# A delta-rule scan and a Fourier mixing block on one core: the first batch put in program order, the weights' conversion rewritten and moved behind it

## The chip, the cores and the metric

The kernel runs on one core of a Trainium2 chip, with one launch. A core has five engines that this text names by the letters of the profile: PE (matrix multiply), PEld (its weight loads, which overlap the multiplies), DVE (vector), ACT (scalar and activation), POOL (GpSimd) and SP (the queue that starts most transfers). The metric is the device time of one execution in microseconds; the kernel before took 895.09 us, the median of three runs (893.43 to 897.38).

## The reference: what is computed

Two blocks, one after the other, all in float32 (the two weight matrices come in as float64).

```python
# block 1, for each of 4 batches and 8 heads, 768 tokens, 48 channels
k_n = k / (norm(k) + 1e-6)
for t in range(768):
    y[t]  = q[t] @ state                       # read before the update
    v_old = state^T k_n[t]
    state = state + beta[t] * outer(k_n[t], v[t] - v_old)
# bridge: heads side by side, x is (4, 768, 384)
# block 2
mixed = real(fft(fft(x, axis=1), axis=2))
u  = x + mixed
un = (u - mean(u)) / sqrt(var(u) + 1e-6)
out = u + relu(un @ w_ch1) @ w_ch2             # w_ch1 384x1536, w_ch2 1536x384
```

## The kernel before

The scan is done in chunks of 64 tokens. Two chunks make a tile g of 128 tokens; a batch has 6 tiles, so there are 24 tiles and 48 steps n of one chunk each. Four tiles make a round; inside a chunk the token-by-token recurrence is replaced by the inverse of a triangular matrix, and a round's 32x32 triangles (32 on each of 128 partitions) are inverted together on DVE. The parts are generators that hand over at each `yield`, so that the main loop can interleave them.

`pre_a(g)` transposes K and forms the products of keys; `invert(r)` inverts a round; `pre_b(g)` prepares the tile's operands; `step(g, c)` carries the state S through one chunk and at a tile's end writes x:

```python
def pre_a(g):
    # four transposes of K on PE, copied to KT by ACT
    # 32 products KT x KT into a PSUM pair, copied by ACT to G and GX
def invert(r):
    nc.gpsimd.memset(M, 0.0)
    nc.vector.transpose(A, G)                            # L286
    nc.scalar.activation(nrm, diag, ACT.Sqrt)            # L292
    for _ in range(2):                                   # two Newton steps of 5 operations
        max, reciprocal, mult, add, times 0.5            # L295 to L299
    ...                                                  # nT, bn with beta, A scaled, L300 to L308
    for j in range(W - 1):                               # W is 32
        nc.vector.tensor_tensor(t, A[...], M[...], op=mult)        # L314
        nc.vector.tensor_tensor(M[...], M[...], t, op=add)         # L317
        yield
    nc.vector.transpose(A, M); nc.vector.transpose(G, M)           # L320, L321
def pre_b(g):
    # Q transposed, copied to QT by ACT; POOL: V times nT, and MT from A        L337 to L343
    # one<-G,GX on PE, XM by ACT; pair<-QT,KT on PE, LQ by DVE                  L356, L368
    # one<-A,XM on PE, into MT by ACT; then WT and U0 from MT, K, V on PE, ACT  L380 to L398
def step(g, c):
    # PE: WT x S;  DVE: U = U0 - that             L416
    # PE: K x U;   DVE: S = S + that (or a copy)  L433, L435
    # at c == 1: x = Q S (ACT, L456) + LQ U (DVE, L465)
```

The weights are turned from float64 into float32 in six pieces of 128x1536 (three of `w1`, three of `w2`), by integer operations on the two words of each number. The buffers carry tags, and a tag's buffers are shared with other parts: `big` (2 buffers) with E and hT, `F` and `O` (1 each) with the Fourier part's F and O3:

```python
def weights():
    nxt = staged(0)                     # a 1.5 MB load into a "big" buffer
    for i, (_, dst) in enumerate(pieces):
        w64 = nxt
        if i + 1 < len(pieces): nxt = staged(i + 1)
        lo, hi = w64[:, :, 0], w64[:, :, 1]
        tmp = wk.tile([128, 2, DFF], I32, tag="F")       # man, exp
        low = wk.tile([128, DFF], I32, tag="O")
        # DVE: man = (hi << 3 & mask) | one               L213, L215
        # DVE: low = lo >> 8; man += low * 2**-44         L217, L218 (two inputs)
        # DVE: exp: shift and mask, subtract and max, min, shift   L222, L224, L226, L227
        # DVE: sign; exp |= sign                          L229, L231 (two inputs)
        nc.gpsimd.tensor_tensor(dst, man, exp, op=mult)  # L232
```

`fourier(b)` and `mlp(b)`:

```python
def fourier(b):
    E = wk.tile([128, 2, TH, DM], F32, tag="big", bufs=2)
    O3 = wk.tile([128, 2, TH, DM], F32, tag="O")
    # for t in 0..2: POOL: E from x tiles t and t+3 (L482, L483); DVE: six folds (L486 to L493)
    F = wk.tile([ND + 1, 4, SEQ], F32, tag="F")
    # pf: 48 products of E and O3 with the tables, copied to F by ACT
    # pb: 24 products of F with dtab, added to x by DVE, mean and variance per tile
def mlp(b):
    for g in range(3):                                   # two tiles of 128 tokens each
        # un = normalised x; transposed by PE (ptr) to unT
        hT = wk.tile([128, KF, GT * 128], F32, tag="big", bufs=2)
        # ph: 36 products with w1, relu by DVE or ACT into hT
        # po: 24 products with w2, added to x by DVE, stored
```

Transfers: K, Q and V come in four transfers a tile and tensor (64 tokens of 4 heads each); K has a ring of 7 tiles; beta comes in 32 transfers a round, started by POOL; the Fourier tables are started by ACT at the very beginning.

The main loop runs before the first step `pre_a` of four tiles, `invert(0)`, `pre_b(0)`, and then 48 steps with the other parts beside them, the weights in the first batch:

```python
for g in range(RL): drain(pre_a(g))
...
drain(invert(0)); load_qv(1); drain(pre_b(0))
side = weights()
for n in range(2 * NLT):
    live = [(step(g, c), 1)]
    # pre_a of the next round in its steps 0 to 3, invert of it in 4 to 6, pre_b(g + 1)
    if b == 0: live.append((part(side, 3), 1))
    ...
    run(live)
    if i == 2 * NL - 1:                 # a batch's last step
        if b == 0: drain(side)
        run([(fourier(b), 1)] + ([(side, 1)] if b > 0 else []))
        side, done = mlp(b), 0
drain(side)
```

The program is not run in the order in which it is written: a scheduler at build time, with times of its own, orders each engine's instructions and gives out the buffers.

Of the kernel before, what the change touches and what calls it, by code (L numbers as in the profile page):

```python
# [11 lines left out]
BF16 = mybir.dt.bfloat16  # L12
# [4 lines left out]
C = 64  # L17
L = 128
# [40 lines left out]
def kernel(  # L59
# [52 lines left out]
    Ks, Qs = [], []  # L112
    for i in range(RING):
        t = const.tile([128, 2, 4, 64], F32, name=f"K{i}")
        nc.gpsimd.memset(t[:, :, :, D:64], 0.0)
        Ks.append(t)
    for i in range(2):
        t = const.tile([128, 2, 4, 64], F32, name=f"Q{i}")
        nc.gpsimd.memset(t[:, :, :, D:64], 0.0)
        Qs.append(t)  # L120
# [3 lines left out]
    def fetch(dst, src, g):  # L124
        b, n = divmod(g, NL)
        for hh in range(2):
            for c in range(2):
                t0 = n * L + c * C
                nc.sync.dma_start(out=dst[hh * C:hh * C + C, c],
                                  in_=src[b, 4 * hh:4 * hh + 4, t0:t0 + C, :].rearrange(  # L130
                                      "j t d -> t j d"))

    def load_k(g):
        if g < NLT:
            fetch(Ks[g % RING][:, :, :, 0:D], k, g)

    def load_qv(g):
        if g < NLT:
            fetch(Qs[g % 2][:, :, :, 0:D], q, g)
            Vs[g] = wk.tile([128, 2, 4, D], F32, tag="V", bufs=2, name="V")  # L140
            fetch(Vs[g], v, g)
# [3 lines left out]
    def load_beta(r):  # L145

        if r * RL >= NLT:
            return
        t = wk.tile([128, W], F32, tag="beta", bufs=2, name="beta")
        for i in range(RL):  # L150
            b, n = divmod(RL * r + i, NL)
            for q4 in range(4):
                hh, blk = divmod(q4, 2)
                p0 = q4 * W + i * 8
                for c in range(2):
                    t0 = n * L + c * C + blk * W
                    nc.gpsimd.dma_start(out=t[p0 + 4 * c:p0 + 4 * c + 4],  # L157
                                        in_=beta[b, 4 * hh:4 * hh + 4, t0:t0 + W])
        betas[r] = t
# [3 lines left out]
    for g in range(RL):  # L163
        load_k(g)
    load_beta(0)
    load_qv(0)
# [9 lines left out]
    nc.scalar.dma_start(out=evt, in_=cn["even"].ap())  # L176
    nc.scalar.dma_start(out=odt, in_=cn["odd"].ap())
    nc.scalar.dma_start(out=dtab, in_=cn["dtab"].ap())

    half_n = const.tile([128, GT], F32, name="half_n")  # L180
    nc.gpsimd.memset(half_n, -0.5)

    def weights():
# [19 lines left out]
        nxt = staged(0)  # L203
        for i, (_, dst) in enumerate(pieces):
            w64 = nxt
            if i + 1 < len(pieces):
                nxt = staged(i + 1)
            lo, hi = w64[:, :, 0], w64[:, :, 1]
            tmp = wk.tile([128, 2, DFF], I32, tag="F", name="wtmp")
            man, exp = tmp[:, 0], tmp[:, 1]  # L210
            low = wk.tile([128, DFF], I32, tag="O", name="wlow")

            nc.vector.tensor_scalar(man, hi, 3, 0x007FFFF8, op0=ALU.logical_shift_left,  # L213
                                    op1=ALU.bitwise_and)
            nc.vector.tensor_scalar(man, man, 0x3F800000, None, op0=ALU.bitwise_or)  # L215
            yield
            nc.vector.tensor_scalar(low, lo, 8, None, op0=ALU.logical_shift_right)  # L217
            nc.vector.scalar_tensor_tensor(man.bitcast(F32), low, 2.0 ** -44, man.bitcast(F32),  # L218
                                           op0=ALU.mult, op1=ALU.add)
            yield  # L220

            nc.vector.tensor_scalar(exp, hi, 20, 0x7FF, op0=ALU.logical_shift_right,  # L222
                                    op1=ALU.bitwise_and)
            nc.vector.tensor_scalar(exp, exp, 896, 0, op0=ALU.subtract, op1=ALU.max)  # L224
            yield
            nc.vector.tensor_scalar(exp, exp, 255, None, op0=ALU.min)  # L226
            nc.vector.tensor_scalar(exp, exp, 23, None, op0=ALU.logical_shift_left)  # L227
            yield
            nc.vector.tensor_scalar(low, hi, 31, 31, op0=ALU.logical_shift_right,  # L229
                                    op1=ALU.logical_shift_left)  # L230
            nc.vector.tensor_tensor(exp, exp, low, op=ALU.bitwise_or)  # L231
            nc.gpsimd.tensor_tensor(dst.rearrange("p c f -> p (c f)"), man.bitcast(F32),  # L232
                                    exp.bitcast(F32), op=ALU.mult)
            yield
# [11 lines left out]
    def pre_a(g):  # L246

        K = Ks[g % RING]
# [3 lines left out]
        for i in range(4):  # L252
            c, jj = divmod(i, 2)
            tr(pt[:, 128 * i:128 * i + 128],
               K[:, c, 2 * jj:2 * jj + 2, :].rearrange("p j d -> p (j d)"), i == 0)
        nc.scalar.activation(KT.rearrange("p c j t -> p (c j t)"), pt, ACT.Copy)
# [5 lines left out]
        for i in range(4):  # L262
            c, jj = divmod(i, 2)
            for q4 in range(4):
                for jp in range(2):
                    hh, blk = divmod(q4, 2)
                    t0 = hh * C
                    rhs = KT[lo[jp], c, jj, t0:t0 + C]
                    if blk:
                        rhs = rhs.rearrange("p (b t) -> p b t", b=2)[:, ::-1, :]  # L270
                    mm(pg[q4 * W:q4 * W + W, jp, C * i:C * i + C],
                       KT[lo[jp], c, jj, t0 + blk * W:t0 + blk * W + W], rhs, i == 0)
# [7 lines left out]
    def invert(r):  # L280
# [10 lines left out]
        diag = A.rearrange(flat)[:, 0:W * W:W + 1]  # L291
        nc.scalar.activation(nrm, diag, ACT.Sqrt)  # L292
        for _ in range(2):

            nc.vector.tensor_scalar(nrm, nrm, 1e-19, None, op0=ALU.max)  # L295
            nc.vector.reciprocal(bn, nrm)
            nc.vector.tensor_tensor(bn, bn, diag, op=ALU.mult)
            nc.vector.tensor_tensor(nrm, nrm, bn, op=ALU.add)
            nc.vector.tensor_scalar(nrm, nrm, 0.5, None, op0=ALU.mult)  # L299
# [25 lines left out]
    def pre_b(g):  # L325

        r, li = divmod(g, RL)
        K, Q, KT, V = Ks[g % RING], Qs[g % 2], KTs.pop(g), Vs.pop(g)
        MTd, Md, nT = rounds[r]
# [3 lines left out]
        for i in range(4):  # L333
            c, jj = divmod(i, 2)
            tr(pt[:, 128 * i:128 * i + 128],
               Q[:, c, 2 * jj:2 * jj + 2, :].rearrange("p j d -> p (j d)"), i == 0)
        nc.scalar.activation(QT.rearrange("p c j t -> p (c j t)"), pt, ACT.Copy)  # L337
# [21 lines left out]
        LQ = wk.tile([128, 2, 4, C], F32, tag="LQ", bufs=2, name="LQ")  # L359
        pl = ps_pair()  # L360
        for i in range(4):
            c, jj = divmod(i, 2)
            for hh in range(2):
                for jp in range(2):
                    t0 = hh * C
                    mm(pl[full[hh], jp, C * i:C * i + C], KT[lo[jp], c, jj, t0:t0 + C],
                       QT[lo[jp], c, jj, t0:t0 + C], i == 0)
        nc.vector.tensor_tensor(  # L368
            LQ.rearrange("p c (jj jp) t -> p jp (c jj) t", jp=2),
            pl[:, :, 0:4 * C].rearrange("p a (i t) -> p a i t", t=C),  # L370
            m_su[:, None, None, :].broadcast_to([128, 2, 4, C]), op=ALU.mult)
# [15 lines left out]
        for c in range(2):  # L387
            for j in range(4):
                for hh in range(2):
# [3 lines left out]
                    mm(pw[full[jp], hh, o:o + C], K[full[hh], c, j, :], mt, c == 0 and jj == 0)  # L393
# [8 lines left out]
    def step(g, c):  # L402
# [18 lines left out]
        if not (n == NL - 1 and c == 1):  # L421
# [3 lines left out]
            for jj in range(2):  # L425
                for jp in range(2):
                    for hh in range(2):
                        mm(pk[full[jp], hh, D * jj:D * jj + D], K[full[hh], c, 2 * jj + jp, :],
# [18 lines left out]
        for j in range(2):  # L447
            for hh in range(2):
                for cc in range(2):
                    for jp in range(2):  # L450
# [3 lines left out]
                        mm(pq[full[cc], jp, o:o + D], QT[lo[jp], cc, j, hh * C:hh * C + C],  # L454
# [154 lines left out]
    for g in range(RL):  # L609
        drain(pre_a(g))  # L610
    for g in range(RL, RING):
        load_k(g)
    load_beta(1)
    drain(invert(0))
    load_qv(1)
    drain(pre_b(0))
# [4 lines left out]
    for n in range(2 * NLT):  # L621
# [3 lines left out]
        last_round = (r + 1) * RL >= NLT  # L625
        live = [(step(g, c), 1)]
        if c == 0:
            if n > 0:
                load_k(g - 1 + RING)
                load_qv(g + 1)  # L630
            if not last_round and ri == 0:
                load_beta(r + 1) if r > 0 else None
        if not last_round:
            nxt = RL * (r + 1)
            if ri in (0, 1, 2):
                live.append((pre_a(nxt + ri), 1))
            elif ri == 3:
                live.append((pre_a(nxt + 3), 1))
                inv = invert(r + 1)
            elif ri < 7:  # L640
                live.append((part(inv, 12), 3))
        if g + 1 < NLT:
            if ri < 6:
                if c == 0:
                    pb = pre_b(g + 1)
                live.append((part(pb, 2 - c), 1))
            elif ri == 7:
                drain(inv) if not last_round else None
                live.append((pre_b(g + 1), 1))
        if b == 0:  # L650
            live.append((part(side, 3), 1))
        elif i < 2 * NL:
# [4 lines left out]
        if i == 2 * NL - 1:  # L657
            if b == 0:
                drain(side)
            f = fourier(b)  # L660
            run([(f, 1)] + ([(side, 1)] if b > 0 else []))
            side, done = mlp(b), 0
# [31 lines left out]
```

## Time and profile before

The execution that was profiled took 892.89 us and its span is 891.1 us.

| | busy us | share of the span |
|---|---|---|
| PE | 689.5 | 77% |
| PEld | 528.7 | 59% |
| DVE | 431.1 | 48% |
| POOL | 217.6 | 24% |
| ACT | 180.1 | 20% |

A busy share is an average over stages that have different limits. The span falls into a first part, in which PE is nearly idle, a middle part, and a long last part in which PE is busy nearly all the time. A table by stage shows this better than the sums do: the same engines' busy times in stretches whose borders are the ends of the steps of the first batch. In the lines of the profile, an instruction's line number is that of the kernel file, and `<-` after a time names what the engine waited for.

### The profile page before, as it was taken

How to read it: one execution, taken by the hardware profiler on the slowest of the kernel's cores; microseconds unless marked ns; L12 is line 12 of the kernel's file. 1: busy time of each engine (PE TensorE's matmuls, PEld its weight loads, DVE VectorE, ACT ScalarE, POOL GpSimd, SP SyncE). 2: the span in 40 equal slices, each digit the busy share in tenths (PEclk: the TensorE clock that was granted, in tenths of full speed). 3: DMA queues.
4: the chain of work that ended last, by engine and by line, in shares of the span. 5: the costliest groups of instructions: out<-in, count | busy, mean ns of one | idle time of the engine just before them, and what ended most of it. 6: DMA issues, size and time to landing. Idle time of an engine off the chain costs nothing. (4 is left out here: it accounts for less than half of the span.)

```text
span 891.1 us, 23482 instructions
## 1 busy us (share of the span) xinstructions
PE 689.5 (77%) x10344; PEld 528.7 (59%) x10344; DVE 431.1 (48%) x1028; ACT 180.1 (20%) x440; POOL 217.6 (24%) x314
## 2 busy tenths in 40 slices
PE   3100003871889999979999999989999999999998
PEld 2100003760678757757878666677777867776775
DVE  0396885288157732596152692249822215241110
ACT  2100001420433123312223223222222211210110
POOL 8957233164218020273010002200111002000000
PEclk9999999955867899988999999999999999999999
DMA  5632210330221011120011111100011000000000
GB/s 112 157 117 71 94 47 7 54 55 1 41 41 19 11 33 39 29 42 15 11 32 29 34 33 33 40 18 4 25 20 42 7 10 10 10 10 18 0 18 18
DMA packets 90584, 31.38 MB, mean 35 GB/s; under 512 B 85010, under 2 KB 88307, under 8 KB 90099
## 3 DMA queue, kind: packets, MB, share of 16 engines
q1 hardware_dynamic: 83808, 28.33, 13.9%
q8 instruction: 81, 1.33, 0.6%
q10 hardware_dynamic: 530, 1.43, 0.5%
q0 software_dynamic: 6144, 0.12, 0.4%
q14 instruction: 21, 0.16, 0.1%
HBM read 25.12 MB, written 4.72 MB: 33 GB/s over the span
## 5 line engine op out<-in xcount | busy, mean ns | idle before, releaser
L104 PE MATMUL ph<-unT,w 128*128 128x256 f32 x864 | 210.9, 396 | 6.4 <-DVE hT L573 2.8
L104 PE MATMUL po<-w,hT 128*128 128x384 f32 x576 | 196.3, 491 | 0.6 <-DVE x L583 0.6
L104 PEld LDWEIGHTS ph<-unT,w 128*128 128x128 f32 x864 | 163.7, 195 | 32.9 <-DVE hT L573 4.4
L104 PEld LDWEIGHTS po<-w,hT 128*128 128x128 f32 x576 | 106.4, 190 | 65.7 <-DVE x L583 0.7
L104 PE MATMUL one<-G,GX 32*32 32x32 f32 x768 | 18.0, 199 | 140.3 <-DVE G L321 140.3
L157 POOL DMA_DIRECT2D beta<-in_beta_dram x192 | 104.8, 554 | 8.5 <-DMA beta<-in_beta_dram 3.6
L104 PEld LDWEIGHTS one<-G,GX 32*32 32x32 f32 x768 | 15.3, 114 | 145.8 <-issue 122.1
L573 DVE TENSOR_SCALAR hT<-ph 128x256 f32<-128x256 f32 x72 | 30.3, 421 | 123.7 <-PE ph L104 123.7
L317 DVE TENSOR_TENSOR M<-M,tmp 128x31 f32<-128x31 f32 (+15 forms) x186 | 68.7, 369 | 4.0
L314 DVE TENSOR_TENSOR tmp<-A,M 128x31 f32<-128x31 f32 (+15 forms) x186 | 68.2, 367 | 4.1
L343 POOL TENSOR_TENSOR MT<-A,pack 128x512 f32<-128x512 f32 x24 | 24.7, 1040 | 156.1 <-PE one L104 98.0
L339 POOL TENSOR_TENSOR V<-V,nT 128x384 f32<-128x384 f32 x24 | 20.0, 837 | 154.2 <-DMA V<-in_v_dram 75.0
L571 ACT ACTIVATE hT<-ph 128x256 f32<-128x256 f32 x72 | 27.6, 383 | 135.8 <-PE ph L104 135.7
L583 DVE TENSOR_TENSOR x<-x,po 128x384 f32<-128x384 f32 x24 | 13.2, 550 | 82.1 <-PE po L104 82.1
L356 ACT ACTIVATE XM<-one 32x256 f32<-32x256 f32 x48 | 18.0, 375 | 164.2 <-PE one L104 163.1
L104 PE MATMUL pair<-MT,K 64*64 64x64 f32 x768 | 45.6, 258 | 2.9 <-ACT MT L380 1.2
L104 PE MATMUL one<-V,MT 64*64 64x48 f32 x768 | 46.9, 236 | 0.0
L104 PEld LDWEIGHTS pair<-MT,K 64*64 64x64 f32 x768 | 40.6, 149 | 6.4 <-issue 3.9
L104 PEld LDWEIGHTS one<-V,MT 64*64 64x64 f32 x768 | 42.9, 155 | 0.3 <-issue 0.2
L435 DVE TENSOR_TENSOR S<-S,pair 128x192 f32<-128x192 f32 x40 | 14.0, 350 | 56.1 <-PE pair L104 56.1
L232 POOL TENSOR_TENSOR w<-wtmp 128x1536 f32<-128x1536 f32 x6 | 25.3, 4216 | 56.7 <-DVE wtmp L231 56.7
L482 POOL TENSOR_TENSOR E<-x 128x384 f32<-128x384 f32 x12 | 12.2, 1020 | 97.1 <-DVE x L465 56.5
(99 smaller groups left out, 918.8 us busy)
## 6 DMA issues: line engine op xcount, KB each, us to landing
w<-in_moe_w_ch_dram SPq DMA_DIRECT2D x6, 1536.0 KB, 6.6
K<-in_k_dram SPq DMA_DIRECT2D x96, 48.0 KB, 2.9
Q<-in_q_dram SPq DMA_DIRECT2D x96, 48.0 KB, 2.5
V<-in_v_dram SPq DMA_DIRECT2D x96, 48.0 KB, 2.4
out_dram<-x SPq DMA_DIRECT2D x24, 192.0 KB, 1.8
beta<-in_beta_dram POOLq DMA_DIRECT2D x192, 0.5 KB, 2.2
evt<-k_even ACTq DMA_DIRECT2D x1, 579.0 KB
odt<-k_odd ACTq DMA_DIRECT2D x1, 576.0 KB, 6.6
```

The lines of the kernel that those rows point to most:

```text
L104: nc.tensor.matmul(o, lhsT=lhsT, rhs=rhs, start=start, stop=stop, skip_group_check=True)
L157: nc.gpsimd.dma_start(out=t[p0 + 4 * c:p0 + 4 * c + 4], in_=beta[b, 4 * hh:4 * hh + 4, t0:t0 + W])
L232: nc.gpsimd.tensor_tensor(dst.rearrange("p c f -> p (c f)"), man.bitcast(F32), exp.bitcast(F32), op=ALU.mult)
L314: nc.vector.tensor_tensor(t, A[:, j + 1:W, j:j + 1].broadcast_to([128, n, j + 1]), M[:, j:j + 1, 0:j + 1].broadcast_to([128, n, j + 1]), o ...
L317: nc.vector.tensor_tensor(M[:, j + 1:W, 0:j + 1], M[:, j + 1:W, 0:j + 1], t, op=ALU.add)
L339: nc.gpsimd.tensor_tensor(V.rearrange("p c j d -> p (c j) d"), V.rearrange("p c j d -> p (c j) d"), nT[:, m8, None].broadcast_to([128, 8, ...
L343: nc.gpsimd.tensor_tensor(MT, MTd[:, m8, None, :].broadcast_to([128, 8, 2, W]), m_blk[:, None, :, None].broadcast_to([128, 8, 2, W]), op=A ...
L356: nc.scalar.activation(XM[rw].rearrange("p m s -> p (m s)"), px[rw, 0:8 * W], ACT.Copy, scale=-1.0)
L435: nc.vector.tensor_tensor(s1v, s0.rearrange("p h j e -> p h (j e)"), pk, op=ALU.add)
L571: nc.scalar.activation(hT[:, fc, :], ph, ACT.Relu)
L573: nc.vector.tensor_scalar(hT[:, fc, :], ph, 0.0, None, op0=ALU.max)
L583: nc.vector.tensor_tensor(x[:, T, :], x[:, T, :], po, op=ALU.add)
```

## The change

It has these parts:

- **Program order.** The first batch, from the first transposes to the end of step 11, is inside a block in which PE, DVE, ACT and POOL run in the order in which the code is written. In the text of that block `pre_b` is split differently (its parts that need no inverse, QT and LQ, come first), and two stages of it run a step earlier at a round's border. The Fourier part of the first batch and all that follows are left to the scheduler.
- **Weights.** The first load is started at step 1, and the conversion of the first three pieces (w1) is put into steps 7 to 11 of the first batch; the other three (w2) come after `fourier(0)`. A piece now takes five DVE operations, two on ACT and one on POOL.
- **Norms.** The two Newton steps lose two operations.
- **Keys twice, in fewer transfers.** A second copy of K, called C (ring of 3), is loaded in one transfer a tile for `pre_a`; Q too takes one. K in the old form has a ring of 3. Beta takes 4 or 8 transfers a round, started by SP. The Fourier tables are started by SP behind the first tiles.

The diff, cut to its core:

```diff
-    def load_k(g): fetch(Ks[g % RING][:, :, :, 0:D], k, g)      # four transfers
+    def load_c(g, engine=None):
+        (engine or nc.sync).dma_start(out=Cs[g % 3][:, :, 0:D], in_=rows(k, g))
+    def load(g):
+        nc.sync.dma_start(out=Qs[g % 2][:, :, 0:D], in_=rows(q, g))
+        halves(Ks[g % 3]..., k, g)
+        halves(Vs[g], v, g)
...
-        for i in range(RL): for q4 in range(4): for c in range(2):
-            nc.gpsimd.dma_start(out=t[p0 + 4 * c:p0 + 4 * c + 4], in_=beta[...])
+        while i < RL: for q4 in range(4):
+            nc.sync.dma_start(out=t[p0:p0 + 8 * m], in_=src)
...
-        nxt = staged(0)
+        w64s = [staged(0), staged(1)]
+        yield
...
-            # ten DVE operations, L213 to L231
+            nc.scalar.activation(man, lo.bitcast(U32), ACT.Copy, scale=2.0 ** -52, bias=1.0)
+            tc.keep_in_program_order(nc.vector.tensor_scalar(num, hi, 0xFFFFF, None, op0=and))
+            nc.vector.scalar_tensor_tensor(man, num, 2.0 ** -20, man, op0=mult, op1=add)
+            yield
+            num = wk.tile([128, DFF], I32, tag="O", name="num")
+            tc.keep_in_program_order(nc.vector.tensor_scalar(num, hi, 20, 0x7FF, ...))
+            nc.scalar.activation(num, num, ACT.Relu, bias=low_e)
+            yield
+            tc.keep_in_program_order(nc.vector.tensor_scalar(num, num, 255, 2.0 ** 23, min, mult))
+            nc.vector.scalar_tensor_tensor(num, hi, -2 ** 31, num, op0=and, op1=or)
+            nc.gpsimd.tensor_tensor(dst, man, num.bitcast(F32), op=mult)
...
-        for _ in range(2): ...                     # invert: five operations twice
+        max, reciprocal, mult, add, reciprocal, mult, scalar_tensor_tensor
...
-            live.append((part(side, 3), 1))
+            if i in (1, 7, 8, 9, 10, 11):
+                live.append((part(side, 1 if i in (1, 11) else 2), 1))
...
+    with tc.manual_schedule(engines={PE, DVE, Activation, Pool}):
+        for g in range(RL): drain(pre_a(g)); load(g) if g < 2
+        # evt, odt, dtab started here, by SP
+        pb = pre_b(0); drain(part(pb, 2)); drain(invert(0)); drain(pb)
+        for n in range(2 * NL): one(n)
+    for b in range(B):
+        f = fourier(b)
+        if b == 0: drain(f); drain(side)
+        else: run([(f, 1), (side, 1)])
+        side, done = mlp(b), 0
+        if b + 1 < B:
+            for n in range(2 * NL * (b + 1), 2 * NL * (b + 2)): one(n)
+    drain(side)
```

## The prediction

> **What bounds the kernel now.** I read the 40 slices first, then asked for the busy times by stage, with borders at the ends of the first batch's steps as the timeline gives them, and then for the timeline of DVE and POOL in the first stages. In the slices, PE and DVE lie side by side:
>
> ```profile
> PE   3100003871889999979999999989999999999998
> DVE  0396885288157732596152692249822215241110
> POOL 8957233164218020273010002200111002000000
> ```
>
> Slices 2 to 6 (22 to 145 us) have no PE at all, while DVE is nearly full. Slices 10 on have PE at 9. So one kernel holds a chain on DVE and then a stretch bound by PE, and a us taken out of the first is a us of the whole as long as PE has nothing else to do there. By stage (length; then busy us and number of instructions on PE, PEld, DVE, ACT, POOL; clock granted to PE; DMA share):
>
> ```profile
> 0.00:24.10 24.10, 10.08 (x276) 7.10 (x276) 0.00 (x0) 5.91 (x13) 20.67 (x52) 1.00 0.52 110
> 24.10:145.90 121.80, 1.34 (x33) 0.94 (x32) 95.11 (x143) 2.38 (x5) 64.19 (x69) 1.00 0.29 88
> 145.90:154.40 8.50, 7.27 (x149) 6.42 (x150) 0.00 (x1) 3.04 (x7) 3.57 (x4) 1.00 0.02 4
> 154.40:197.50 43.10, 36.74 (x1260) 31.35 (x1260) 22.20 (x62) 16.33 (x39) 13.43 (x23) 0.77 0.34 57
> 197.50:229.90 32.40, 8.80 (x154) 7.33 (x155) 21.89 (x51) 3.00 (x7) 13.51 (x21) 0.51 0.03 4
> 229.90:256.90 27.00, 23.56 (x819) 20.44 (x818) 7.62 (x17) 10.86 (x26) 4.64 (x5) 0.75 0.30 51
> 256.90:288.50 31.60, 27.52 (x318) 24.43 (x305) 24.16 (x79) 10.54 (x30) 19.78 (x36) 0.76 0.17 27
> 288.50:891.10 602.60, 574.19 (x7358) 430.67 (x7358) 260.15 (x678) 128.00 (x317) 77.78 (x108) 0.98 0.10 22
> ```
>
> In order: first `pre_a`; `invert(0)`; `pre_b(0)`; steps 0 to 7; the wait for `invert(1)` and `pre_b(4)`; steps 8 to 11; `fourier(0)`; and from the first ph product everything else, PE busy 95% of 602.6 us. The waits name the link that holds the second stage:
>
> ```profile
> ACT XM L356 <- PE one L104: 147.9, 3, 120.6
> PE one L104 <- DVE G L321: 135.7, 2, 119.9
> POOL w L232 <- DVE wtmp L231: 56.7, 5, 12.2
> ```
>
> PE waited 119.9 us for L321, the last operation of `invert(0)`. DVE's timeline shows why that took so long: between any two dependent operations of the inversion stands one of the conversion.
>
> ```profile
> 55.23 0.95 DVE L217 TENSOR_SCALAR wlow<-w 128x1536 int32<-128x1536 int32 x1
> 56.09 0.29 DVE L314 TENSOR_TENSOR tmp<-A,M 128x135 f32<-128x135 f32 x1
> 56.41 3.40 DVE L317 TENSOR_TENSOR M<-M,tmp 128x135 f32<-128x135 f32 x1
> 59.85 0.32 DVE L314 TENSOR_TENSOR tmp<-A,M 128x156 f32<-128x156 f32 x1
> ```
>
> The columns are start, duration, engine, line. Besides, DVE stood idle in it: 11.6 us for the first weights to land ahead of an operation that the inversion then had to queue behind, and 13.9 us for POOL's multiply.
>
> **What the Trainium skill says.** "VectorE: DVE Perf Modes", section "The perf-mode tier table (the rule you actually need)": a one-input tensor_scalar in fp32 from and to SBUF goes at twice the rate of a two-input operation. The trace agrees: 949 ns against 1749 ns for 1536 elements. "SBUF — State Buffer", section "Who interferes with whom": GpSimd and DVE share a port pair, two-input DVE operations contend with GpSimd reads, and whoever issues first blocks the other. The trace agrees: the 3.40 us above, for a form that takes 0.29 us elsewhere, falls into POOL's multiply of 4.46 us that began at 55.20. "ScalarE: Activation LUTs", section "What ACT_TABLE_LOAD costs": 186 ns + 0.833 ns an element, some 93 ns more with a pointer bias. For 512 elements that is 0.61 us and the trace has 0.60, so my estimate for the two new ACT operations on 1536 elements is 1.47 and 1.56 us. "DMA: Bandwidth & Descriptors", section "Issuing engines are not separate DMA queues": transfers of all queues interleave on the same 16 engines. The trace agrees at the start: while the two large tables come over ACT's queue, from 2 to 8 us, the DMA engines are full and the first keys, issued from 0.7 us, release PE only at 8.66.
>
> **The change, part by part.** All stages below are those of the table.
>
> *Head, 24.1 us.* The tables move behind the keys, and a tile's keys come in one transfer. PE's program order is now transposes, 32 products, transposes, and so on; from the trace such a round takes 1.1 (transposes) + 0.6 (KT) + 1.2 (products) and about 0.4 of hand-over, 3.3 us; four are 13 us. With the first keys at some 5 us that ends at 18; QT and LQ now stand on DVE ahead of the inversion's first transpose, another 3.5. I take **21.5** (-2.6). The beta transfers (POOL 104.8 us busy for 192) wait for nobody on this path: no gain but tidiness.
>
> *invert(0), 121.8 us.* Undisturbed it can be read from `invert(1)`: its columns 15 to 30 run from 205.60 to 217.73 with nothing between, 12.1 us; columns 0 to 14 have the same sizes as 30 to 16, so 12.1 less the 0.9 of column 15, 11.2; the two last transposes take to 221.45, 3.7. The beginning took from 24.14 to 32.08, 7.9, less LQ 0.5 and the two dropped operations 0.4, is 7.0. Sum **34.0** (-87.8). This is the change's main term.
>
> *pre_b(0)*: the same chain of PE, ACT, PE, **8.5**.
>
> *Steps 0 to 7 and the border to step 8, 43.1 + 32.4 = 75.5 us.* Before, a tile's two steps took 11.7 to 12.6 us. After, steps 0 to 3 take 24; then `invert(1)` is written into steps 4 to 6, 34 us of DVE plus about 4 for the steps' own DVE operations; then step 7 and the rest of `pre_b(4)`, 10. **72** (-3.5): here program order gives almost nothing, since the scheduler had overlapped the same two things.
>
> *Steps 8 to 11, 27.0 us.* Three pieces come in. A piece costs DVE 3 x 0.95 + 2 x 1.75 = 6.35 us (before 8 x 0.95 + 2 x 1.75 = 11.1), ACT 3.0, POOL about 4.3. Three are 19 us of DVE beside 7.6, in fixed order, so a state update can stand behind 2.7 us of conversion, and V and MT on POOL behind a multiply. **33** (+6, my choice; it could be 3 or 15).
>
> *fourier(0) to the last pb product, 256.9 to 285.8, 28.9 us.* Before, two of three E pairs were done while steps still ran. After, POOL has all six E operations (1.0 us each) behind the multiply of the third piece: some 7 us more; PE at a better clock gives perhaps 3 back. **33** (+4).
>
> *The other three pieces.* Their `man` and `num` need the tags F and O, so they begin when pb has finished with F; one buffer each, so they run one after the other: 9 us of ACT and DVE and 4.3 of POOL, 13.5 a piece. hT needs a `big` buffer, and in the new order it comes after the second of these pieces: 13.5 + 9 = 22.5 us after the last pb. Before, the first ph came 2.7 us after it. In the gap PE can do the two ph groups that fit in PSUM and some 6 us of the second batch. Loss against before: 22.5 - 2.7 - 6, about 14, and 2 for po that waits for the last piece: **2.7 + 16**.
>
> *The rest*: the same PE work, 574 us of 602.6, **602.6**. The second copy of the keys is 24 x 192 KB on DMA engines that are 10% busy there.
>
> Sum: 21.5 + 34.0 + 8.5 + 72 + 33 + 33 + 18.7 + 602.6 = 823.3 us of span. The median before is 4.0 above the profiled span, so **827 us**, 7.6% less.
>
> **The rivals.** *The weights become the new wait.* The conversion is moved, not removed, and stands where PE could start its long stretch. For it: F, O and `big` are shared, DVE was 24.2 of 31.6 us busy in the Fourier stage already, and w1's pieces sit in steps whose every DVE operation is on the chain. If all six pieces' 13.5 us came to stand on the path, that is 81 us in place of the 26 that I count (6 + 4 + 16), 882; with half of that excess, 855. Against it: w1 needs only to be ready by the first ph, and PE has other work in part of the gap. *The gain is larger.* If steps 8 to 11 hide w1 and the second batch fills the gap, the terms +6, +4 and +16 shrink to some 5 together: about 806; and if the long stretch gains from less waiting in its 28 us without PE, below 800. *Program order stalls.* In a fixed order each engine waits for the operation that happens to be next; steps 0 to 7 have about 40 such hand-overs on each of PE and DVE, and 0.5 us lost on each would be 20 us, 847. The trace speaks mildly against it: the chains of steps 0 to 3 were already bound by dependences, PE 36.7 of 43.1 us busy. *A transfer blocks.* SP issues all loads in one order, and a weights' load or a V waiting for its buffer holds back what is behind it; the page has SP waiting 106 us for PE in the first 300, without harm to the chain. *PE's clock*: 0.5 to 0.8 in the steps, whatever the order; I leave it.
>
> **Range and chances.** No rival eats 88 us alone; two of the bad ones together leave about 860, the good one gives 800. Range **798 to 858**. Faster by over 2% (below 877): **0.95**; within 2%: **0.04**; slower: **0.01**.
>
> **What would show it right or wrong.** Right: L326 and L327, the end of `invert(0)`, at about 55 us with no gaps between its columns; the first S at about 64; the last x of the first batch near 170; a gap on PE after the last pb that ends with hT and names DVE; the long stretch again near 600 us. Wrong in a step: the first S later than 72 (the head or hand-overs), more than 40 us for steps 8 to 11 (conversion on the chain), ph starting late with POOL or DMA named (buffers), or a long stretch that is off by more than 15 us, on which I have assumed nothing changes.

## The result, and the profile after

The changed kernel takes **839.8 us** (median of four executions, 837.9 to 843.2) beside 894.3 for the kernel before: ratio 0.940, 95% interval [0.935, 0.945]. A second set of six gave 838.0 (833.7 to 844.3), 0.939 [0.936, 0.943]. Predicted were 827, range 798 to 858. The page of the profile (span 836.1) has these slices:

```profile
PE   5039436669577999889999999899999999999998
DVE  0951694767998127952427921599513123431110
POOL 1012002440413000230000111200100020000000
PEclk9999655557569899999999999999999999999999
```

The slices without PE have shrunk from four (the third to the sixth; the prediction wrote 2 to 6) to one (the second, 21 to 42 us; the third already has PE at 3), and POOL, which had 5 to 9 in its first four slices, is nearly idle. PE's granted clock stands at 5 to 7 from the fifth slice to the twelfth, the steps and the Fourier stage, where the table before had 0.51 to 0.77. By stage, with the columns of the table before (length; busy us and count on PE, PEld, DVE, ACT, POOL; clock; DMA share; GB/s):

```profile
0.00:19.77 19.77, 11.14 (x308) 8.30 (x308) 0.61 (x2) 8.18 (x15) 2.33 (x15) 1.00 0.71 112
19.77:53.84 34.07, 0.00 (x0) 0.00 (x0) 31.17 (x80) 0.26 (x1) 2.58 (x3) 1.00 0.50 159
53.84:62.33 8.49, 6.38 (x145) 5.76 (x146) 0.01 (x2) 2.48 (x6) 1.08 (x2) 1.00 0.01 3
62.33:126.31 63.98, 36.19 (x1184) 31.30 (x1184) 39.23 (x101) 16.08 (x38) 6.41 (x7) 0.75 0.28 51
126.31:139.41 13.10, 8.74 (x225) 7.84 (x226) 5.33 (x7) 6.14 (x9) 0.95 (x1) 0.50 0.05 9
139.41:175.20 35.79, 24.66 (x720) 21.65 (x720) 24.68 (x23) 16.60 (x28) 15.11 (x9) 0.60 0.57 146
175.20:212.68 37.48, 31.07 (x379) 27.61 (x376) 28.25 (x78) 9.72 (x28) 8.32 (x10) 0.68 0.24 63
212.68:216.23 3.55, 1.55 (x8) 0.75 (x6) 2.47 (x9) 2.68 (x4) 1.78 (x3) 0.50 0.23 46
216.23:239.33 23.10, 10.68 (x172) 8.57 (x172) 23.03 (x37) 6.34 (x6) 7.42 (x4) 0.57 0.25 77
239.33:836.10 596.77, 566.66 (x7218) 426.68 (x7218) 261.46 (x651) 129.02 (x317) 65.72 (x71) 0.98 0.12 26
```

In order: head; `invert(0)`; `pre_b(0)`; steps 0 to 7 up to the end of `invert(1)`; the border to step 8; steps 8 to 11; `fourier(0)`; last pb to first ph; first ph to first hT; the rest. In the second row DVE is busy 31.17 of 34.07 us, with 80 operations where 143 stood before. DVE's timeline shows the columns of the inversion with nothing between them (start, duration, engine, line):

```profile
28.90 0.30 DVE L320 TENSOR_TENSOR tmp<-A,M 128x135 f32<-128x135 f32 x1
29.23 0.30 DVE L323 TENSOR_TENSOR M<-M,tmp 128x135 f32<-128x135 f32 x1
29.57 0.32 DVE L320 TENSOR_TENSOR tmp<-A,M 128x156 f32<-128x156 f32 x1
29.92 0.32 DVE L323 TENSOR_TENSOR M<-M,tmp 128x156 f32<-128x156 f32 x1
```

The same two sizes stood 3.76 us apart before (56.09 to 59.85) and stand 0.67 apart now. The waits confirm it:

```profile
ACT XM L376 <- PE one L104: 106.8, 20, 33.1
POOL w L237 <- DVE num L235: 57.3, 6, 15.1
PE one L104 <- DVE G L327: 45.2, 4, 34.9
```

PE waits at most 34.9 us for the end of an inversion, in place of 119.9. POOL's wait for the conversion has not gone: it moved with it. The stages side by side (us; the fifth column is a second trace of the changed kernel, span 831.9, the last two are experiments below):

| stage | before | predicted | after | after, 2nd | no conversion | no fixed order |
|---|---|---|---|---|---|---|
| head | 24.1 | 21.5 | 19.8 | 19.6 | 19.8 | 13.7 |
| invert(0) | 121.8 | 34.0 | 34.1 | 34.1 | 34.0 | 35.2 |
| pre_b(0) | 8.5 | 8.5 | 8.5 | 8.5 | 8.5 | 8.5 |
| steps 0–7, border | 75.5 | 72 | 77.1 | 77.1 | 74.4 | 74.5 |
| steps 8–11 | 27.0 | 33 | 35.8 | 33.6 | 22.5 | 30.7 |
| fourier(0) | 28.9 | 33 | 37.5 | 33.1 | 28.1 | 36.4 |
| last pb to first hT | 5.7 | 22.5 | 26.7 | 26.7 | 5.7 | 26.7 |
| rest | 599.6 | 598.8 | 596.8 | 599.2 | 599.0 | 592.6 |

(The prediction's 18.7 + 602.6 = 621.3 is split here by its own 22.5 us from pb to hT.) The two traces of the changed kernel agree within 0.2 us except in steps 8 to 11, in `fourier(0)` and in the rest. In the first two of these the clock granted to PE differed (0.60 and 0.68 in the first trace, 0.70 and 0.85 in the second), and so did a DVE operation beside POOL in each: L223 took 4.35 us at the longest in the first trace and 1.74 in the second, and the first L493 took 4.18 and 1.33. Which of the two made the difference is not shown. Differences of 4 us in those stages are no evidence of anything.

### The profile page after: what moved, and what is told of

The parts are those of the page before. It is cut to its first block, busy times and chain, and to the rows that moved or that the text cites. A ratio compares the mean times of both kernels' runs of the same rounds, so it can differ in the third digit from the quotient of the medians.

```text
span 836.1 us, 23182 instructions
## 1 busy us (share of the span) xinstructions
PE 697.1 (83%) x10344; PEld 538.5 (64%) x10344; DVE 416.2 (50%) x980; ACT 197.5 (24%) x452; POOL 111.7 (13%) x122
## 3 DMA queue, kind: packets, MB, share of 16 engines
q8 instruction: 81, 1.33, 0.7%
## 4 chain that ended last, share of the span: by engine, by line
PE 58%; DVE 28%; issue 4%; ACT 3%; POOL 2%; SPq 2%; DMA 1%; DVEq 0%; ACTq 0%; POOLq 0%
PE ph L104 18%; PE po L104 17%; PE pair L104 9%; DVE tmp L320 7%; DVE M L323 7%; PE one L104 5%; PE pf L104 3%; PE pb L104 3%; PE one L107 3%; SPq L136 1%; DVE A L326 1%; DVE G L327 1%; DVE A L291 1%; DVE O L493 1%; POOL w L237 1%
## 5 line engine op out<-in xcount | busy, mean ns | idle before, releaser
L320 DVE TENSOR_TENSOR tmp<-A,M 128x31 f32<-128x31 f32 (+15 forms) x186 | 70.3, 378 | 5.0
L323 DVE TENSOR_TENSOR M<-M,tmp 128x31 f32<-128x31 f32 (+15 forms) x186 | 68.0, 365 | 5.1
L104 PEld LDWEIGHTS pair<-U,K 64*64 64x64 f32 x704 | 16.9, 150 | 33.1 <-DVE U L423 16.6
L104 PE MATMUL pair<-U,K 64*64 64x48 f32 x704 | 23.3, 245 | 16.2 <-DVE U L423 15.1
L104 PE MATMUL pair<-KT 48*32 48x64 f32 x1536 | 23.1, 249 | 11.8 <-DVE S L442 8.6
```

What stands on the lines that cost most here:

```text
L104: nc.tensor.matmul(o, lhsT=lhsT, rhs=rhs, start=start, stop=stop, skip_group_check=True)
L320: nc.vector.tensor_tensor(t, A[:, j + 1:W, j:j + 1].broadcast_to([128, n, j + 1]), M[:, j:j + 1, 0:j + 1].broadcast_to([128, n, j + 1]), o ...
L323: nc.vector.tensor_tensor(M[:, j + 1:W, 0:j + 1], M[:, j + 1:W, 0:j + 1], t, op=ALU.add)
```

## The experiments

Theory A is the prediction's: what is gained is the freed inversion, and the conversion, moved, costs again where it now stands. The rivals were that the fixed program order is itself a gain or a loss, and that the cheaper writing or the transfers do the work.

**1. Moving alone.** The kernel before, with the old conversion written later:

```diff
 # one step of batch 0
-            live.append((part(side, 3), 1))
+            if i >= 7:
+                live.append((part(side, 3), 1))
 # after the steps
+            f = fourier(b)
             if b == 0:
+                drain(f)
                 drain(side)
-            f = fourier(b)
-            run([(f, 1)] + ([(side, 1)] if b > 0 else []))
+            else:
+                run([(f, 1), (side, 1)])
```

> The kernel before, with the old conversion written into steps 7 to 11 (three pieces) and behind fourier(0) (three), and nothing else changed. In the built program the scheduler has put the first three pieces into invert(0) all the same. Theory A (the time comes from DVE's inversion being free of the conversion, by whatever means): invert(0) takes some 34 + 33 + 12 for the first load = 80 us in place of 122, and some 25 us are given back behind fourier(0): about 880. Theory B (program order on all engines brings the gain): 895. Theory C (writing the conversion later is enough): about 840.

Measured: 896.4 us, ratio 1.0024 [1.0002, 1.0047]. Writing it later does not hold it there: the scheduler still placed the three w1 pieces in the inversion, which took 85.7 us. The rows of the inversion and of the rest:

```profile
24.32:109.97 85.65, 1.29 (x33) 0.94 (x32) 71.58 (x113) 2.33 (x4) 50.82 (x67) 1.00 0.30 88
274.20:894.60 620.40, 580.17 (x7330) 433.75 (x7330) 274.41 (x685) 128.20 (x317) 82.39 (x103) 0.96 0.10 21
```

The inversion is 36 us shorter than before, and all of it came back at the MLP's start: from the last pb to the first hT 25.5 us in place of 5.7, and the rest 20.8 longer. The total is the figure of theory B, but run 4 shows that its reason, the fixed order, is not what brings the gain. Theory A's mechanism was right, and its 25 us of loss behind `fourier(0)` were 41.

**2 and 3. The new conversion alone.** The kernel before with the new five DVE operations a piece, without and with the marks that keep one of them in each third at its written place:

```diff
-tc.keep_in_program_order(nc.vector.tensor_scalar(num, hi, 0xFFFFF, ...))   # twice more alike
+nc.vector.tensor_scalar(num, hi, 0xFFFFF, ...)                             # run 2; run 3 keeps the marks
```

> The kernel before with the new conversion in the place of the old, and nothing that holds it back; the built program has all six pieces in invert(0). Theory A: invert(0) takes 34 + 6 x 6.35 = 72, and 12 for the first load and some 8 of waits for POOL: 92 in place of 122, so about 865. Theory B: 895. Theory D (the cheaper conversion is the main thing): below 850.

> As e2, but three of a piece's five DVE operations are marked to keep their program order; the rest of the kernel is left to the scheduler. In the built program the inversion stands alone and the six pieces lie in steps 0 to 8, all ahead of fourier(0). Theory A: invert(0) 34 us, steps longer by perhaps 20 us, nothing behind fourier(0): 820 to 835, at least as good as the changed kernel. Theory B: above 870.

Measured: 861.4 us, 0.963 [0.956, 0.970], without marks, near theory A's 865; 856.9, 0.957 [0.952, 0.962], with them. Without marks the inversion took 85.6 us, with four pieces and most of the fifth in it; the sixth began 7 us behind its end. With them the inversion took 42.8, and steps 0 to 7 with the border grew from 75.5 to 116.4: 41 us, 6.8 a piece, for pieces of 6.35 us of DVE. So theory A's 820 to 835 missed: the steps hide next to nothing. Part of the loss is not the five operations but POOL's multiply. Four DVE operations of the second inversion, which take 0.2 to 0.4 us elsewhere, took 3.3, 4.2, 6.0 and 3.5 us beside a multiply. The longest, and then POOL:

```profile
146.55 6.00 DVE L311 TENSOR_TENSOR tmp<-A,M 128x207 f32<-128x207 f32 x1
```

```profile
146.97 3.43 POOL L229 TENSOR_TENSOR w<-man,num 128x1536 f32<-128x1536 f32 x1
150.35 1.00 POOL L479 TENSOR_TENSOR E<-x 128x384 f32<-128x384 f32 x1
151.31 0.99 POOL L480 TENSOR_TENSOR E<-x 128x384 f32<-128x384 f32 x1
```

That the inversion took 42.8 and not 34 has a cause of its own, seen in the waits of run 3 and in POOL's timeline:

```profile
DVE M L305 <- POOL M L282: 6.4, 1, 6.4
```

```profile
23.82 14.28 POOL L157 DMA_DIRECT2D beta<-in_beta_dram  x28
38.09 0.97 POOL L282 MEMSET M<- 128x1024 f32 x1
```

POOL issues 28 beta transfers in 14.28 us, and the memset that the inversion needs stands behind them. In the kernel before, the memset stood behind 32 such transfers, too (37.81 us), but DVE was then waiting 11.6 us for the first weights, and so it did not show.

**4. No fixed order.** The changed kernel without its block:

```diff
-    with tc.manual_schedule(engines=engines):
+    with ExitStack():
```

> The changed kernel without the block of program order: the scheduler orders all of it; the three marked operations of a piece stay. The built program has the inversion alone. Theory A: 835 to 850, invert(0) still 34 us. Theory B: most of the 55 us gone, above 870.

Measured: 822.3 us, 0.919 [0.913, 0.925], below the changed kernel's interval. Both theories had the block as neutral or a gain; program order on all engines is a cost, 16 to 18 us (838.0 and 839.8 less 822.3). Six of them lie in the head. PE's timeline there, in the changed kernel:

```profile
6.30 1.19 PE L104 MATMUL pair<-KT 48*32 48x64 f32 x64 [0.69 <-ACT KT L260]
7.41 1.11 PE L107 MATMUL one<-pack,C 128*128 128x128 f32 x4
9.21 1.18 PE L104 MATMUL pair<-KT 48*32 48x64 f32 x64 [0.69 <-ACT KT L260]
```

and without the block:

```profile
7.35 2.06 PE L104 MATMUL pair<-KT 48*32 48x64 f32 x128
9.34 1.97 PE L107 MATMUL one<-pack,C 128*128 128x128 f32 x8
11.24 2.01 PE L104 MATMUL pair<-KT 48*32 48x64 f32 x128
```

In written order each tile's products wait 0.69 us for the copy of its own transposes; a round is 2.92 us. The scheduler does the transposes of two tiles together and waits for neither. The other 10 to 12 us are spread: 2.6 in the steps up to the border, 3 to 5 in steps 8 to 11, 4 to 7 in the rest, less 1.1 in the inversion; on `fourier(0)` the two traces of the changed kernel disagree. The shares of steps 8 to 11 and of the rest are rough: the two traces of the changed kernel alone differ there by 2.2 and 2.4 us.

**5. No conversion.** The changed kernel with the weights' loads and conversion left out (both weights filled with 0.02):

```diff
     def weights():
-        (loads and six pieces)
+        return
+    nc.gpsimd.memset(w1, 0.02); nc.gpsimd.memset(w2, 0.02)
```

> The changed kernel with the weights' loads and their conversion left out (both weights are filled with 0.02 by two memsets on POOL at the start), so the difference from the changed kernel is what the moved conversion still costs and where. Theory A (the conversion costs where it was put, and the buffers it holds cost the MLP's start): inversion 34 as in the changed kernel, steps 0 to 7 with the border 72 in place of 77, steps 8 to 11 27 in place of 36, Fourier 31 in place of 37.5, first hT 6 us after the last pb in place of 27, together about 800 us (795 to 806). Rival B (part of the slow steps 8 to 11 and of the Fourier stage is program order or PE's clock, not the conversion): these two stages stay at 33 and 36, and the whole comes to 810 to 815.

Measured: 796.7 us, 0.892 [0.888, 0.896]. Its rows for steps 8 to 11 and `fourier(0)`:

```profile
136.73:159.19 22.46, 20.60 (x728) 17.19 (x728) 7.43 (x19) 10.25 (x24) 5.84 (x6) 0.87 0.50 86
159.19:187.32 28.13, 25.55 (x371) 23.16 (x365) 21.00 (x65) 9.58 (x28) 4.64 (x7) 0.81 0.14 26
```

Theory A holds in the whole, and rival B's 33 and 36 us for these two stages do not: the conversion with its loads still costs 838.0 − 796.7 = 41 us, 6.9 a piece, a little more than its 6.35 us of DVE. It lies in the steps up to the border (3), steps 8 to 11 (11 to 13), the Fourier stage (5 to 9) and the start of the MLP (21).

**6. The multiply on DVE.**

```diff
-            nc.gpsimd.tensor_tensor(dst..., man, num.bitcast(F32), op=ALU.mult)
+            nc.vector.tensor_tensor(dst..., man, num.bitcast(F32), op=ALU.mult)
```

> The changed kernel with the last operation of each piece, the multiply, on DVE in place of POOL. Theory A (the piece is a serial chain, and POOL's 3.5 us both lengthen it and slow the DVE operations beside it, L223 from 0.95 to as much as 4.35 us): the 23.1 us from ph to hT become 19 to 20, steps 8 to 11 lose 1 to 3 us and the Fourier stage 2 to 4, since E no longer stands behind a multiply on POOL; 831 to 834 us. Rival B (DVE is the scarce engine in these stages): each piece puts 1.75 us more on the path, 845 to 849 us.

Measured: 824.3 us, 0.922 [0.918, 0.926]: 14 us less than the changed kernel, about twice what theory A gave, although DVE has 1.75 us more to do a piece. What POOL did to DVE is seen in the changed kernel, DVE first and then POOL:

```profile
159.71 4.35 DVE L223 TENSOR_SCALAR num<-w 128x1536 int32<-128x1536 int32 x1 [1.64 <-POOL w L237]
```

```profile
156.13 3.55 POOL L237 TENSOR_TENSOR w<-man,num 128x1536 f32<-128x1536 f32 x1 [8.29 <-DVE num L235]
159.61 0.86 POOL L359 TENSOR_TENSOR V<-V,nT 128x384 f32<-128x384 f32 x1
160.39 1.07 POOL L363 TENSOR_TENSOR MT<-A,pack 128x512 f32<-128x512 f32 x1
161.39 0.86 POOL L359 TENSOR_TENSOR V<-V,nT 128x384 f32<-128x384 f32 x1
162.18 1.07 POOL L363 TENSOR_TENSOR MT<-A,pack 128x512 f32<-128x512 f32 x1
```

L223 takes 0.95 us elsewhere. First it waits for the multiply, whose input buffer it overwrites, and then it takes 4.35 us beside two V and two MT, which had queued behind the multiply and run for 3.6 us without a gap. The second trace has the wait but not the long operation:

```profile
159.10 1.57 DVE L223 TENSOR_SCALAR num<-w 128x1536 int32<-128x1536 int32 x1 [2.00 <-POOL w L237]
160.78 2.40 DVE L225 SCALAR_TENSOR_TENSOR man<-num,man 128x1536 f32<-128x1536 int32 x1
```

There L225 took 2.40 in place of 1.76 us, and on POOL an MT took 1.75 and a V 2.34. What repeats in both traces are the multiplies behind `fourier(0)`: a column operation of 0.4 us beside each took 3.3 to 3.5 us. The profiled execution of run 6 was 10 us longer than its others, so its stages (31.7 and 31.9 us in steps 8 to 11 and Fourier, 21.1 from ph to hT) cannot be set beside those of the other runs; where the 14 us came from, stage by stage, is not shown.

**7. hT before the last two pieces.** (The pieces are counted from 0.)

```diff
             drain(f)
-            drain(side)
+            advance(side, 3)              # piece 3; the load of piece 5 is staged later, too
+            first = mlp(b); advance(first, 2)
+            drain(side)
```

> The changed kernel with the first group's transposes and its hT asked for after piece 3 of the weights in place of after piece 5, and with the sixth load staged after it, so that hT does not stand behind the second w2 piece for one of the two big buffers. Theory A (the 23 us before the first hT are a wait for a buffer): hT at about 226 in place of 239, and 10 to 13 us off the whole, 827 to 830 us. Rival B (po needs all of w2, so the MLP is held by the three pieces themselves): hT comes earlier but PE idles later by as much, 836 to 841 us.

Measured: 830.4 us, 0.933 [0.926, 0.940]. The first hT came 13.3 us after the last pb in place of 26.7, so the wait was one for a buffer; but the rest took 604.0 us, 5 to 7 more. The net is some 8 us, and its interval overlaps the changed kernel's: between theory A and B.

**8. LQ behind the inversion.**

```diff
-        pb = pre_b(0); drain(part(pb, 2)); drain(invert(0)); drain(pb)
+        drain(invert(0)); pb = pre_b(0); drain(pb)
```

> The changed kernel with the first tile's Q transposes and LQ written behind the inversion again, in place of ahead of it; all else, program order too, as it was. Theory A (in a fixed order the inversion's first transpose waits for the LQ product, and so for Q's transfer): the first transpose starts at 14 in place of 19.8 us, the stage behind the inversion grows from 8.5 to 11 or 12 us, and the whole loses 2 to 3 us, 837 us. Rival B (the head is bound by the keys' transfers and the four rounds of PE whatever stands behind them): the first transpose stays at 18 to 20 us and the whole is 840 to 843 us.

Measured: 833.6 us, 0.934 [0.929, 0.938], not separable from the changed kernel. The stages are clear: the head 16.5 in place of 19.6 to 19.8, against rival B's 18 to 20, and the stage behind the inversion 8.5, unchanged, against theory A's 11 or 12. So LQ ahead of the inversion costs 3.2 us and saves nothing; the other 2.8 of the head's 6 are the 0.69 us waits.

**9. The changed kernel again.**

> The changed kernel itself once more, on the chip and beside the runs of the three kernels that follow, to know how far its time moves between chips. Theory A (the time repeats): 838 to 843 us, and the gains read from the multiply on DVE, the early hT and the late LQ are what they seem. Rival B (its granted clock differs from chip to chip, as steps 8 to 11 at 35.8 us and the Fourier stage at 37.5, against 33.6 and 33 to 34 in two of those kernels, hint): 830 to 836 us, and those gains shrink by as much.

Measured: 838.0 us. Theory A: the time repeats, and the gains of runs 4 and 6 stand. Rival B was right only in that the two stages differ.

**10. The old writing in the new places.** The changed kernel with the old conversion:

```diff
-            (two operations on ACT, three tensor_scalar and two scalar_tensor_tensor on DVE)
+            (eight tensor_scalar, one scalar_tensor_tensor and one tensor_tensor on DVE)
```

> The changed kernel with the old writing of the conversion, eight one-input and two two-input DVE operations a piece in place of three and two, nothing on ACT, at the same places and in three parts as the new one. Theory A (nearly every us that the conversion takes on DVE ahead of the MLP stands on the path, wherever it is put): 11.1 less 6.35 is 4.75 us a piece, six pieces 28 us, 864 to 870 us. Rival B (DVE has room in these stages, 24.7 of 35.8 us busy in steps 8 to 11, and the new writing pays for its ACT operations with hand-overs): 845 to 855 us.

Measured: 857.3 us, 0.960 [0.957, 0.963]: 19 us more than the changed kernel for 28 us more of DVE work, between the two theories. The border is 3 us shorter (no ACT operation of the conversion stands ahead of the step's own), steps 8 to 11 take 39.4, and in the wait for hT PE finds 12 matmuls to do in place of 172. The rest takes 617.9 us in place of 596.8 and 599.2, and that is where nearly all of the net loss lies.

**11 and 12. Putting it together.** Run 11 has the edits of runs 4, 6 and 7. Run 12 has hT ahead of all three w2 pieces, and stages the last two loads later:

```diff
-            if 0 < i < len(pieces) - 2:
+            if 0 < i < 3:
                 w64s.append(staged(i + 1))
...
             drain(f)
-            advance(side, 3)
             first = mlp(b); advance(first, 2)
             drain(side)
```

> The changed kernel without the block that fixes program order, with the piece's multiply on DVE and with hT asked for after piece 3 of the weights. Theory A (the three gains are separate: order about 17 us, multiply some 8, hT some 8): 805 to 810 us. Rival B (multiply and hT shorten the same 23 us and the scheduler gives part back): 812 to 818 us.

> As the run before it, but with all three pieces of w2 behind the first hT, and the loads of the last two behind it too. Theory A (the ph products, about 26 us of PE, cover the conversion of w2): first hT within 5 us of the first ph, and 796 to 804 us. Rival B (po then waits for the third w2 piece, which comes some 47 us after the last pb because two loads stand in the chain): PE idles later instead, and the time is that of the run before or up to 10 us more.

Measured: 817.6 us, 0.915 [0.912, 0.919], and 819.0, 0.918 [0.914, 0.921]. Both are faster than both kernels of the case; neither is separable from run 4. The totals are rival B's in both: the gains overlap. Set beside run 4, run 11 has its first hT 13.4 us sooner after the last pb (13.3 in place of 26.7) and a rest that is 12.8 longer (605.4 in place of 592.6). Run 12 shows how, in PE's waits from 205 to 290 us and in ACT's timeline:

```profile
PE po L104 <- DVE w L239: 11.7, 2, 10.5
```

```profile
238.88 1.64 ACT L224 ACTIVATE man<-w 128x1536 f32<-128x1536 uint32 x1 [8.47 <-DMA w<-in_moe_w_ch_dram]
```

The first hT starts 3 us after ph, PE spends 19 us on its ph products (I had put 26), and then po waits 10.5 us for the last piece of w2, which itself waited 8.5 us for its load. The MLP needs all weights, and something waits for the last of them.

## Why the prediction was right, and where it was off

The main term was right to 0.1 us: `invert(0)` 34.1 against 34.0, taken from the undisturbed `invert(1)`; its three parts came out as worked out, too (6.9 to the first column, 23.4 for the columns, 3.7 for the last transposes). The Newton steps went from ten operations to seven, so three were dropped and not two. `pre_b(0)` was right too. They make 87.7 us of gain; everything else gave 28 to 33 back. The landmarks came where they were put, a little later each: the inversion's end at 53.8 (about 55), the first S at 62.3 (64), the last x at 175.2 and 172.8 (near 170), and the gap on PE behind the last pb ends with hT. The wait on PE itself names ACT, which writes hT, and ACT had waited for DVE's L235, the last reader of the `big` buffer. DVE first, then ACT:

```profile
237.49 1.75 DVE L235 SCALAR_TENSOR_TENSOR num<-w,num 128x1536 int32<-128x1536 int32 x1
```

```profile
239.33 0.38 ACT L578 ACTIVATE hT<-ph 128x256 f32<-128x256 f32 x1 [3.09 <-DVE num L235]
```

In the prediction's own steps:

- *Head*, 21.5 against 19.6 to 19.8. A round is 2.92 us, not 3.3. LQ's 3.5 us were right (3.2 in run 8). I took its place ahead of the inversion as given and did not ask what it buys: nothing.
- *Beta: "no gain but tidiness"*. Half wrong. Before, POOL's issues did not matter; with the inversion freed they do, 6.4 us in run 3. Without this part of the change the main term would probably not have been 34; no run has the changed kernel with beta on POOL. I judged the wait in the old schedule, where a longer one covered it.
- *Steps 0 to 7 and the border*, 72 against 77.1. Run 5 splits the miss: 2.7 are conversion, for two thirds of a piece already stand at step 7, where I counted none; 2.4 are a sum drawn too tight.
- *Steps 8 to 11*, 33 against 35.8 and 33.6; *Fourier*, 33 against 37.5 and 33.1. The totals fit the second trace, but the first is two errors that cancel: without conversion steps 8 to 11 take 22.5 (run 5), not 27, and the conversion costs 11 to 13, not 6. That 33 came so near is luck. Run 5 has 728 matmuls in this stage where the kernel before had 819, and a clock of 0.87 where it had 0.75; which of the two makes the 4.5 us is not shown.
- *The other three pieces*, 22.5 us from pb to hT against 26.7. A piece takes 13.4 us as worked out (L223 at 217.09 and again at 230.51). What I left out is that DVE was still busy with the tail of `fourier(0)` and a column of the next inversion until 217.1, 4.4 us after the last pb. PE was busy for 10.7 us in the gap, 5.1 of it with the two ph groups, so the 6 us counted for the second batch came out, and the rest took 2.0 us less than the sum had (0.4 more in the second trace).

These are the whole miss: −1.7 (head), +0.1, +5.1 (steps), +2.8, +4.5 (Fourier), +4.2 (gap), −2.0 (rest) add up, within rounding, to the 12.8 us by which the span of 836.1 exceeds the sum of 823.3.

The rival *program order stalls* was put at 20 us, held unlikely, and looked for in steps 0 to 7. It was real, 16 to 18 us, but only 2.6 of it lay in the steps. The prediction's mild evidence (PE 36.7 of 43.1 us busy) came from a schedule whose order the scheduler had chosen. The rival *the weights become the new wait* was right in kind: 6.9 us a piece, half of the 13.5 of its worst case, and 41 us in all where the prediction counted 26. What the fixed order buys, the conversion held out of the inversion, the three marked operations a piece do alone: in run 4 the inversion takes 35.2 us without the block.

So of the 56 us: the new conversion with its marks, put in the old program, is worth 37 (run 3); the transfers, the order of loads, the later places, the split of `pre_b` and the shorter norms together 35 more (run 4 against run 3); and the fixed order takes 16 back. No run takes these 35 apart, but the stages of the two traces, 36.7 us apart in span, say where they lie: 11.0 in the head, 7.5 in the inversion and 9.9 in the rest. Steps 0 to 7 with the border lost 42.0, and 33.9 of that came back in steps 8 to 11, in `fourier(0)` and in the wait for hT. So in these stages the later places, if it is they that moved the 42.0, were worth some 8 us.

## What to carry to other kernels

Work taken off a serial chain is not gone: before counting the gain, ask on which engine it runs and whether that engine has free time anywhere ahead of its deadline; here six pieces of 6.35 us of DVE cost some 7 us each in the steps or around the MLP's start, and 7.7 in run 2, where most of them stood in the inversion (set beside run 3's 42.8 us for the inversion and the 75.5 for the steps, run 2 takes 46 us more up to step 8). To hold work out of a chain, mark the few operations that matter and leave the others to the scheduler. And after the longest wait is gone, look again at every wait that it used to cover, and at a slow engine's operation that both delays and slows a faster one.

## What the runs showed of the hardware

- A DVE operation could last as long as the POOL operations beside it, and not only as long as one of them: 6.0 us in place of 0.4 beside a multiply and two E operations (run 3), 4.35 in place of 0.95 beside two V and two MT (first trace of the changed kernel). It need not: in the second trace the same one took 1.57, and POOL's operations were slowed with it (MT 1.75, V 2.34 us). Beside the 3.5 us multiply DVE operations took 3.47 (L320) and 3.42 us (L323), in place of about 0.4. Moving the multiply to DVE, which was the busier engine, was worth 14 us.
- The two ACT operations on 1536 elements took 1.58 to 1.63 us (L222, from every second uint32 word) and 1.57 to 1.58 (L231) in the changed kernel; the estimates were 1.47 and 1.56.
- PE's granted clock did not set the length of the chain of `pre_b(0)`: it took 8.5 us at a clock of 1.00 in the kernel before (149 matmuls, PE busy 7.3) and 8.5 at 0.50 without the block (149, busy 7.4). In steps 8 to 11 the clock was 0.87 without the conversion and 0.60 to 0.70 with it; whether a sparser PE is granted less, or something else decides it, these runs do not settle.
